# Moving the mixer's stages between the head slots of a fused attention, mixer and FFN kernel

## The chip, the cores and the metric

One core of one Trainium2 chip runs the whole program. The metric is the device time of one execution in microseconds; the profile gives the span from the program's first to its last instruction beside it. An execution is compared with another one of the same chip, and a time of several runs is their median.

## The reference, cut to what matters

2048 tokens of 576 features are normalized (xn) and go down two ways. Way A is attention of 32 heads over the last 512 keys of a cache, with an output projection. Way B is a mixer (layernorm, a product with w1, gelu, a shift of four column groups by one or two tokens, a product with w2, residual) and then an FFN of 4608 hidden features. The output is x + s · silu(B).

```
xn = _layernorm(x)
s  = attention(xn, k_cache, v_cache, wq, wo)          # 32 heads, 512 keys, softmax, then @ wo
h  = gelu(_layernorm(xn) @ w1)                        # mixer, first stage
hs = shift(h) @ w2                                    # mixer, last stage: groups shifted by 1, -1, 2, -2 tokens
x1 = xn + hs
h2 = gelu(_layernorm(x1) @ w3) @ w4                   # FFN
out = x + s * silu(x1 + h2)
```

## The kernel before, in words

The tokens are cut into four blocks of 512 (b = 0 to 3, NB = 4). The attention part runs through 128 slots, u = 32·b + head; the main loop from L742 on writes the order of TensorE, SyncE (SP) and GpSimd (POOL) out by hand (`manual_schedule` with these three engines). What VectorE (DVE) and ScalarE (ACT) do, and in which order, is set by the tile framework's planner, which also places instructions that stand outside of such a region into an engine's order where it finds them free to go; `high_priority` lifts some DVE and ACT work.

A slot u holds, in this order on TensorE: a score product `stage_s(u, 0)` (L459, 128x512), the query projection of the next head `stage_q(u+1)` (L439; in every fourth slot, `trip`, also four half products of `rest_q`, L425, and `stage_s(u, 1)` moves ahead of them), then what `fill[u]` holds, then three more rounds: `stage_s(u, i)`, half of `stage_v(u-1)` for i = 1 and 2 (eight products po of 129 columns, L476), and a third of the slot's list of extra matmuls, `pe_fill[u]`. At the slot's end `stage_t(u-1)` issues the DMA transpose of head u-1's output on SP (L489, o to oT). A slot with an empty `pe_fill` is called bare here.

Beside the heads a block needs these steps:

- `load_x` (POOL), `ln1_steps` (DVE, three steps a slot through `later`) and four DMA transposes `tr1` (SP, L392) that fill `xT_b[b % 2]`, which `stage_q` of the block's first head reads one slot ahead of the block.
- `ln2_steps` (DVE, writes `xnn_b`) and four DMA transposes `tr2` (SP, L392) that fill `xnnT`, the input of the mixer's first stage.
- `b1(b, c)`, c = 0 to 4: five matmuls each (L552, into ph), then a gelu of six DVE instructions with a tanh on ACT between them (L567 to L575). Chunk 4 also copies two border columns to and from the neighbouring block.
- `b2_shift` (DVE, L592), `b2(b, tt)`, tt = 0 to 3 (five matmuls each, L603, then a DVE add L614), and `b2_rem` (twenty matmuls of 64 columns, an add L628, and the store of the block's x1 to `x1_dram` on SP, L630).
- `wo_atoms(b)`: the block's output projection, five groups of matmuls over the 32 heads' oT (L500): four of 32 with 512 columns, one of 128 with 64 columns. Groups of blocks 0 to 2 lie in five slots of the next block, those of block 3 behind the last slot.
- `load_x1(0)`, `ln3_steps(0)` and `ln3_transpose(0)` (SP, L206): FFN's first layernorm, for block 0.

`x1_pool` has two buffers. They hold, one after another, key staging, x of blocks 2 and 3, the scaled attention output of blocks 0 to 2 on its way to `s_dram`, each block's x1 until its store, and the x1 that the FFN loads back (`load_x1`, L196). `xnn_b`, `xnnT`, `hs` and the gelu's three temporaries have one buffer each; `hb` has two, as have the banks `pq` that psq, ph and psx1r share.

The FFN (from L765 on) has TensorE, DVE and ACT ordered by hand. Its weight loads `load_w` (nine slabs of four DMAs on SP, L788 to L793) are tied behind the last head's transpose; `load_sx(0)` and `load_x1(1)` come after them in the program, and `ln3_work(1)`, the layernorm of FFN block 1, is handed out step by step to the DVE between the FFN's own steps (`pop`), from the first round on.

```
        with tc.issue_after(last_t[0].ins):
            for i in range(NSL):
                load_w(i)
...
        load_sx(0)
        load_x1(1)
        work = ln3_work(1)
```

Where the steps stood before, by slot (counted within 0 to 127; base = 32·b):

| step | block 0 | block 1 | block 2 | block 3 |
|---|---|---|---|---|
| ln2 from | 7 | 35 | 67 | 99 |
| tr2 | 28, 29, 30, 31 | 39, 39, 40, 40 | 71, 71, 72, 72 | 103, 103, 104, 104 |
| b1 chunks 0 to 4 | 33, 34, 36, 37, 38 | 42, 44, 45, 46, 48 | 74, 76, 77, 78, 80 | 106, 108, 109, 110, 112 |
| b2 tiles 0 to 3 | 50, 52, 53, 54 | 82, 84, 85, 86 | 114, 116, 117, 118 | 120, 121, 122, 124 |
| ln1 from (for that block) | before the loop | 19 | 55 | 87 |
| output projection | 34 to 38 | 65 to 69 | 97 to 101 | behind 127 |

ln3 of block 0 began in slot 121 and its transposes stood in slot 125.

Of the kernel before, what the change touches and what calls it, by code (L numbers as in the profile page):

```python
# [31 lines left out]
def kernel(  # L32
# [14 lines left out]
    nc = tc.nc  # L47
# [15 lines left out]
    NB = S // QB  # L63
# [140 lines left out]
    def ln3_transpose(b):  # L204
        for tt in range(TB):
            nc.sync.dma_start(out=xT_b[b % 2][:, :, tt * P:(tt + 1) * P], in_=xm_b[b % 2][:, tt, :], transpose=True)  # L206

    with ExitStack() as actx:
# [99 lines left out]
        def late(ap, fn):  # L308
            g = nc.gpsimd.tensor_copy(out=gate[:, :], in_=ap)
            with tc.issue_after(g.ins):  # L310
                fn()
# [272 lines left out]
        def b2_shift(b):  # L584
            with tc.high_priority(offset=HP):
                b2_shift_(b)
# [79 lines left out]
        def later(u, make, per):  # L666
            cell = []
            for i in range(2 * TB + 1):
                def step(i=i):
                    if not cell:  # L670
                        cell.append(make())
                    cell[0][i]()
                at(u + i // per, step)

        def trip(u):
            return Hq - 1 <= u < U - 1 and u % 4 == 3

        for b in range(NB):
            base = b * Hq
            if b > 0:  # L680
                for i, group in enumerate(wo_atoms(b - 1)):
                    pe(base + (2 if b == 1 else 1) + i, group)
            later(base + (7 if b == 0 else 3), lambda b=b: ln2_steps(b), 3)
            for tt in range(TB):
                at(base + (28 + tt if b == 0 else 7 + tt // 2), lambda b=b, tt=tt: tr2(b, tt))
            for c, u in enumerate((33, 34, 36, 37, 38) if b == 0 else (10, 12, 13, 14, 16)):
                pe(base + u, b1(b, c))
            for bb in ([b - 1] if b > 0 else []) + ([b] if b == NB - 1 else []):
                o2 = base + (24 if bb == b else 18)
                at(o2 - 1, lambda bb=bb: b2_shift(bb))  # L690
                tiles = [o2 + i for i in range(TB + 1) if not trip(o2 + i)][0:TB]
                for tt, u in enumerate(tiles):
                    pe(u, b2(bb, tt))
                pe(tiles[-1], b2_rem(bb))
            if b + 1 < NB:
                at(base + (14 if b == 0 else 4), lambda b=b: late(pT_t[b * Hq + (14 if b == 0 else 4)][0][0:1, 0:1],
                                                                 lambda: load_x(b + 1, nc.gpsimd)))
                u1 = base + (23 if b else 19)
                later(u1, lambda b=b: ln1_steps(b + 1), 3)
                for tt in range(TB):  # L700
                    at(u1 + (3 + tt // 2 if b else 5 + tt), lambda b=b, tt=tt: tr1(b + 1, tt))
# [17 lines left out]
        for b in range(NB):  # L719
            at((b + 1) * Hq + 1, lambda b=b: row_range(b))  # L720
        at(3 * Hq + 10, lambda: load_x1(0))
        later(3 * Hq + 25, lambda: ln3_steps(0), 3)
        at(3 * Hq + 29, lambda: ln3_transpose(0))
        at(U + 2, finish_flag)

        with tc.manual_schedule(engines={SP, POOL, PE}):
# [456 lines left out]
```

## Time and profile before

| | |
|---|---|
| median of 3 runs | 845.85 us (843.45, 845.85, 849.34) |
| the profiled execution's own time | 844.12 us |
| its span | 842.3 us |
| granted TensorE clock, mean | 0.999 |
| slots 0 to 127 | 11.4 to 517.7 us of the span |
| output projection of block 3 | 519.3 to 552.5 us |
| FFN | 552.5 us to the end |

In a line of the timeline stand the start in us, the time from the first start to the last end of the merged instructions, the engine, the line of the kernel, the operation, what it writes and reads, the count, and in brackets the idle time before it with what ended it. Consecutive instructions of one kind are one line. Matmuls overlap each other, so what one costs is read from one start to the next and not from its length. `SPq` and `POOLq` are issues of DMAs; the time of an issue is not that of its transfer. A line of windows gives the busy time of each engine in a stretch. DMA lines give the median time from issue to landing.

### The profile page before, as it was taken

Reading aid. Unit: us, or ns where it says so; the run is one execution under the profiler, and the core shown is the slowest. Engines: PE = TensorE matmul, PEld = TensorE weight load, DVE = VectorE, ACT = ScalarE, POOL = GpSimd, SP = SyncE. Lnnn points to the kernel's source line nnn. Section 1 sums busy time; section 2 is a strip of 40 time slices with the busy share of each in tenths; the row PEclk is TensorE's granted clock in tenths of the full one; section 3 lists DMA queues with packets and bytes.
Section 4 is the critical chain, followed back from the end, with each engine's and each line's share of the span. In section 5 each row is a group of like instructions: output and inputs, shape, how many; then the busy total and the mean of one; then the engine's idle time right before and its main releaser. Section 6 shows DMA issues by size and latency. Waiting matters only on the chain.

```text
span 842.3 us, 19541 instructions
## 1 busy us (share of the span) xinstructions
PE 827.3 (98%) x7971; PEld 476.4 (57%) x7971; DVE 474.0 (56%) x1430; ACT 451.3 (54%) x806; POOL 92.2 (11%) x157
## 2 busy tenths in 40 slices
PE   8999999999999999999999999999999999999997
PEld 5666654655664555565465555455555555555555
DVE  5878655568762458683448775034246636555333
ACT  6777753478793388794367865033233333334610
POOL 3242313001010110110011000000000000000000
PEclk9999999999999999999999999999999999999999
DMA  7997963263371183463065236993001321230101
GB/s 187 197 169 181 194 173 73 63 104 95 95 135 45 42 155 67 108 122 80 19 110 127 68 94 126 275 344 61 2 2 44 63 70 44 45 88 16 44 15 46
DMA packets 140752, 83.95 MB, mean 100 GB/s; under 512 B 107328, under 2 KB 133632, under 8 KB 140656
## 3 DMA queue, kind: packets, MB, share of 16 engines
q1 hardware_dynamic: 130048, 53.01, 30.7%
q0 software_dynamic: 9216, 28.15, 12.1%
q8 instruction: 64, 1.05, 0.6%
q10 hardware_dynamic: 1392, 1.48, 0.5%
q14 instruction: 32, 0.26, 0.1%
HBM read 49.17 MB, written 9.44 MB: 70 GB/s over the span
## 4 chain that ended last, share of the span: by engine, by line


## 5 line engine op out<-in xcount | busy, mean ns | idle before, releaser
L461 ACT ACTIVATE pT<-sc 128x512 bf16<-128x512 f32 x512 | 289.3, 597 | 127.3 <-PE sc L459 118.3
L459 PE MATMUL sc<-qT,kT 128*128 128x512 bf16 x512 | 178.5, 378 | 1.4 <-DVE qT L449 0.6
L476 PEld LDWEIGHTS <-pT 128*128 128x128 bf16 x2048 | 137.7, 98 | 55.3 <-issue 8.9
L476 PE MATMUL po<-v_sb,pT 128*128 128x129 bf16 x2048 | 162.0, 220 | 0.4 <-ACT pT L461 0.4
L439 PE MATMUL psq<-xT_b,wq_b 128*128 128x512 bf16 x544 | 138.3, 379 | 0.3 <-DVE xT_b L405 0.3
L834 PE MATMUL ph<-xT_b,w_s 64*128 64x512 bf16 x976 | 127.1, 376 | 0.0
L871 PE MATMUL pm<-w_s,h 64*128 64x512 bf16 x864 | 122.3, 377 | 0.0
L500 PE MATMUL pswo<-wo_sb,oT 128*128 128x512 bf16 x512 | 116.7, 379 | 1.6 <-DMA oT<-o 1.6
L481 DVE TENSOR_TENSOR o<-po,ri_b 128x256 bf16<-128x256 f32 x256 | 108.1, 422 | 6.6
L852 ACT ACTIVATE h<-ph 128x512 bf16<-128x512 f32 x67 | 39.4, 597 | 130.5 <-PE ph L834 130.5
L871 PEld LDWEIGHTS <-h 64*128 64x128 bf16 x1728 | 70.8, 94 | 55.5 <-issue 0.4
L500 PEld LDWEIGHTS <-oT 128*128 128x128 bf16 x1024 | 65.1, 98 | 58.0 <-DMA oT<-o 2.1
L871 PE MATMUL pr<-w_s,h 64*128 64x64 bf16 x864 | 90.2, 189 | 0.2 <-ACT h L852 0.2
L439 PEld LDWEIGHTS <-wq_b 128*128 128x128 bf16 x544 | 52.8, 97 | 64.0 <-issue 3.4
L834 PEld LDWEIGHTS <-w_s 64*128 64x128 bf16 x1152 | 57.1, 94 | 48.3 <-issue 0.2
L850 DVE COPY hx<-ph 128x512 f32<-128x512 f32 x55 | 38.0, 691 | 69.3 <-PE ph L834 69.3
L480 DVE RECIPROCAL ri_b<-po 128x2 f32<-128x2 f32 x256 | 42.7, 167 | 53.0 <-PE po L476 48.8
L449 DVE CAST qT<-psq 128x512 bf16<-128x512 f32 x56 | 38.6, 690 | 49.0 <-PE psq L425 29.4
L447 DVE TENSOR_TENSOR qT<-psq,rq 128x512 bf16<-128x512 f32 x48 | 33.2, 691 | 52.6 <-ACT pT L461 32.2
L459 PEld LDWEIGHTS <-kT 128*128 128x128 bf16 x512 | 47.3, 97 | 27.1 <-DVE qT L449 0.6
L264 POOL DMA_DIRECT2D wq_b<-in_A_wq_dram x30 | 23.3, 776 | 303.5 <-PE sc L459 275.0
L824 DVE TENSOR_SCALAR fence<-ph,ph 1x1 f32<-1x1 f32 x61 | 12.8, 209 | 49.7 <-PE ph L834 49.1
(146 smaller groups left out, 739.7 us busy)
## 6 DMA issues: line engine op xcount, KB each, us to landing
wq_b<-in_A_wq_dram POOLq DMA_DIRECT2D x30, 512.0 KB, 4.6
w_s<-in_B_w_dram SPq DMA_DIRECT2D x9, 576.0 KB, 7.1
wo_sb<-in_A_wo_dram POOLq DMA_DIRECT2D x8, 576.0 KB, 5.2
w_s<-in_B_w_dram SPq DMA_DIRECT2D x9, 512.0 KB, 7.2
x_dram<-x SPq DMA_DIRECT2D x4, 576.0 KB, 3.6
x<-x_dram SPq DMA_DIRECT2D x4, 576.0 KB, 4.8
s_b<-s_dram SPq DMA_DIRECT2D x4, 576.0 KB, 5.2
x_b<-in_A_x_dram SPq DMA_DIRECT2D x4, 576.0 KB, 6.1
```

The costliest lines, as they stand in the source:

```text
L439: nc.tensor.matmul(psq[:, :], lhsT=w[:, kc, hh * Dh:(hh + 1) * Dh], rhs=xT_b[qb % 2][:, kc, :], start=(kc == 0 and not (qb and hh == 1)), ...
L449: nc.vector.tensor_copy(out=qT[:, :], in_=psq[:, :])
L459: nc.tensor.matmul(sc[:, :], lhsT=kT[:, g, kc * P:(kc + 1) * P], rhs=qT_t[u][:, :], start=True, stop=True)
L461: nc.scalar.activation(out=pT[:, :], in_=sc[:, :], func=ACT.Exp, scale=SCALE)
L476: nc.tensor.matmul(po[:, j, :], lhsT=pTs[kc][:, tt * P:(tt + 1) * P], rhs=v_sb[:, g, kc, 0:Dh + 1], start=(kc == 0), stop=(kc == KCH - 1))
L480: nc.vector.reciprocal(out=ri, in_=po[:, :, Dh])
L481: nc.vector.tensor_tensor(out=o[:, t0:t0 + 2, :], in0=po[:, :, 0:Dh], in1=ri.unsqueeze(2).to_broadcast([P, 2, Dh]), op=ALU.mult)
L500: nc.tensor.matmul(ps, lhsT=oT_t[qb * Hq + h][:, tt, :], rhs=wo_sb[:, h, lo:hi], start=(h == 0), stop=(h == Hq - 1))
L834: nc.tensor.matmul(ps[i][:, :], lhsT=lhsT, rhs=xT[half, kc, :], start=first, stop=last, skip_group_check=True)
L850: nc.vector.tensor_copy(out=src[:, :], in_=ps[i][:, :])
L852: nc.scalar.activation(out=h3[:, :], in_=src[:, :], func=ACT.Gelu_apprx_tanh)
L871: nc.tensor.matmul(out, lhsT=h3_t[b, fc][half, tt * P:(tt + 1) * P], rhs=w4_s[fc // WS][half, fc % WS, lo:hi], start=key not in started, s ...
```

## The change

The arithmetic and all matmuls stay; only the slots change. `pe` gets three lists for the mixer's first stage and the output projection, so that a chunk can stand ahead of a projection group in its slot ("early") or behind it ("after"):

| step | block 0 | block 1 | block 2 | block 3 |
|---|---|---|---|---|
| ln2 from | 7 | 35 | 60 | 85 |
| tr2 | 27, 28, 29, 30 | 39, 39, 40, 40 | 63, 63, 64, 64 | 89, 89, 90, 90 |
| b1 chunks 0 to 4 | 34, 36, 36, 37, 37 | 44, 45, 46, 48, 49 | 65, 66, 66, 68, 68 | 97, 98, 98, 100, 100 |
| b2 tiles 0 to 3 | 52, 53, 54, 56 | 72, 73, 74, 76 | 104, 105, 106, 108 | 124, 125, 126, 127 |
| ln1 from (for that block) | before the loop | 19 | 56 | 80 |
| output projection | 34 to 38 | 65 to 69 | 97 to 101 | behind 127 |

tr1 of blocks 2 and 3 moves with ln1 (three and four slots behind its begin). In slot 27 the first tr2 now stands ahead of the last tr1 of block 1. ln3 of block 0 begins in slot 116 and its transposes stand in slot 120. The loads of x stay in slots 14, 36 and 68, `load_x1(0)` in slot 106.

```diff
+        ln2_at = (7, Hq + 3, 2 * Hq - 4, 2 * Hq + 21)
+        tr2_at = ((27, 28, 29, 30), (Hq + 7, Hq + 7, Hq + 8, Hq + 8),
+                  (2 * Hq - 1, 2 * Hq - 1, 2 * Hq, 2 * Hq), (2 * Hq + 25, 2 * Hq + 25, 2 * Hq + 26, 2 * Hq + 26))
+        b1_early = {Hq + 2: [(0, 0)], Hq + 4: [(0, 1)], Hq + 5: [(0, 3)]}
+        b1_after = {Hq + 4: [(0, 2)], Hq + 5: [(0, 4)]}
+        for b in range(2, NB):
+            base = b * Hq
+            b1_early.update({base + 2: [(b, 1)], base + 4: [(b, 3)]})
+            b1_after.update({base + 1: [(b, 0)], base + 2: [(b, 2)], base + 4: [(b, 4)]})
+        for c, u in enumerate((12, 13, 14, 16, 17)):
+            b1_after[Hq + u] = [(1, c)]
+        b2_at = ((Hq + 20, Hq + 21, Hq + 22, Hq + 24), (2 * Hq + 8, 2 * Hq + 9, 2 * Hq + 10, 2 * Hq + 12),
+                 (3 * Hq + 8, 3 * Hq + 9, 3 * Hq + 10, 3 * Hq + 12), (4 * Hq - 4, 4 * Hq - 3, 4 * Hq - 2, 4 * Hq - 1))
+        x_at = (14, Hq + 4, 2 * Hq + 4)
+        ln1_at = (19, Hq + 24, 2 * Hq + 16)
...
+        for u, chunks in b1_early.items():
+            for b, c in chunks:
+                pe(u, b1(b, c))
+        for b in range(1, NB):
+            for i, group in enumerate(wo_atoms(b - 1)):
+                pe(b * Hq + (2 if b == 1 else 1) + i, group)
+        for u, chunks in b1_after.items():
+            for b, c in chunks:
+                pe(u, b1(b, c))
...
-        later(3 * Hq + 25, lambda: ln3_steps(0), 3)
-        at(3 * Hq + 29, lambda: ln3_transpose(0))
+        later(3 * Hq + 20, lambda: ln3_steps(0), 3)
+        at(3 * Hq + 24, lambda: ln3_transpose(0))
```

The loop over the blocks below it keeps its calls of `later`, `at` and `pe` and takes their slots from these tables.

More of the change, by code (lines that the diff above doesn't have):

```diff
@@ L676, in trip @@
             return Hq - 1 <= u < U - 1 and u % 4 == 3
-        for b in range(NB):
[L679 to L683, printed above, removed]
-            for tt in range(TB):
[L685 to L694, printed above, removed]
+        ln2_at = (7, Hq + 3, 2 * Hq - 4, 2 * Hq + 21)
@@ new lines @@
+        for b in range(1, NB):
[4 more added lines that the diff above has]
+                pe(u, b1(b, c))
+        for b in range(NB):
+            later(ln2_at[b], lambda b=b: ln2_steps(b), 3)
+            for tt in range(TB):
+                at(tr2_at[b][tt], lambda b=b, tt=tt: tr2(b, tt))
+            at(b2_at[b][0] - 1, lambda b=b: b2_shift(b))
+            for tt in range(TB):
+                pe(b2_at[b][tt], b2(b, tt))
+            pe(b2_at[b][TB - 1], b2_rem(b))
@@ L695 @@
             if b + 1 < NB:
-                at(base + (14 if b == 0 else 4), lambda b=b: late(pT_t[b * Hq + (14 if b == 0 else 4)][0][0:1, 0:1],
-                                                                 lambda: load_x(b + 1, nc.gpsimd)))
-                u1 = base + (23 if b else 19)
+                at(x_at[b], lambda b=b: late(pT_t[x_at[b]][0][0:1, 0:1], lambda: load_x(b + 1, nc.gpsimd)))
+                u1 = ln1_at[b]
                 later(u1, lambda b=b: ln1_steps(b + 1), 3)
```

## The prediction, made before the change was run

> **What bounds the kernel now.** I read the page's first part, then the timeline of TensorE (PE) for its idle places, then SP's queue and the DVE around each of them.
>
> ```profile
> span 842.3 us, 19541 instructions
> PE 827.3 (98%) x7971; PEld 476.4 (57%) x7971; DVE 474.0 (56%) x1430; ACT 451.3 (54%) x806; POOL 92.2 (11%) x157
> ```
>
> TensorE is busy for 98% of the span, and the change keeps every matmul. So it can only win the time in which PE waits, and it can lose wherever it makes PE wait anew. The 98% alone wouldn't prove that, since matmuls overlap; the starts do. In the timeline of PE, below, one line with eight po products is followed 0.47 us later (516.97 to 517.44) by a score product, and that one 0.21 us later by the next. These are the undisturbed steps against which I read the waits.
>
> [...]
>
> ```profile
> 110.50 0.63 PE L476 MATMUL po<-v_sb,pT 128*128 128x129 bf16 x8
> 112.70 0.38 PE L552 MATMUL ph<-xnnT,w_sb 128*128 128x512 bf16 x1 [1.57 <-DMA xnnT<-xnn_b]
> ...
> 174.23 0.63 PE L476 MATMUL po<-v_sb,pT 128*128 128x129 bf16 x8
> 175.96 0.39 PE L552 MATMUL ph<-xnnT,w_sb 128*128 128x512 bf16 x1 [1.10 <-DMA xnnT<-xnn_b]
> ...
> 180.57 0.63 PE L476 MATMUL po<-v_sb,pT 128*128 128x129 bf16 x8
> 181.29 0.86 PE L459 MATMUL sc<-qT,kT 128*128 128x512 bf16 x2
> ...
> 314.48 0.86 PE L459 MATMUL sc<-qT,kT 128*128 128x512 bf16 x2
> ...
> 447.48 0.86 PE L459 MATMUL sc<-qT,kT 128*128 128x512 bf16 x2
> ...
> 516.04 0.88 PE L476 MATMUL po<-v_sb,pT 128*128 128x129 bf16 x8
> ...
> 516.97 0.63 PE L476 MATMUL po<-v_sb,pT 128*128 128x129 bf16 x8
> 517.44 0.38 PE L459 MATMUL sc<-qT,kT 128*128 128x512 bf16 x1
> 517.65 0.49 PE L476 MATMUL po<-v_sb,pT 128*128 128x129 bf16 x3
> 518.50 0.94 PE L476 MATMUL po<-v_sb,pT 128*128 128x129 bf16 x13 [0.36 <-ACT pT L461]
> 519.28 1.02 PE L500 MATMUL pswo<-wo_sb,oT 128*128 128x512 bf16 x4
> ...
> 524.67 1.03 PE L500 MATMUL pswo<-wo_sb,oT 128*128 128x512 bf16 x4
> 527.33 1.04 PE L500 MATMUL pswo<-wo_sb,oT 128*128 128x512 bf16 x4 [1.63 <-DMA oT<-o]
> ```
>
> From these starts: chunk (0,0) in slot 33 waits 1.73 us (112.70 less 110.97) for the transposes of xnnT; chunk (1,0) in slot 42 waits 1.26; slot 43 loses 0.25 before its third score product and 0.28 before its fourth, and slots 75 and 107 show the same long pair of score products (0.86 where an undisturbed pair takes 0.59), 0.53 each time; the last slot loses 0.25 and 0.67, together 0.92, to ACT's exps; and the last projection waits 1.80 (527.33 less 525.53) for the last head's oT. Together 7.3 us are there to be won.
>
> **The change part by part.**
>
> Block 0's first stage. tr2 goes one slot earlier, chunk (0,0) one slot later (34), so PE comes for xnnT about 2.7 us later, a bare slot (four of them, one longer, take the 11.31 us of the window below), and would come 0.9 us after the data even if the transposes landed no sooner. The 1.73 us go. The price is on SP: in slot 27 the first tr2 passes ahead of the last tr1, which `stage_q(32)` needs in slot 31. One issue is 1.3 us (2.52 for two, below). I take 0, as that transpose is issued four slots ahead; bounds 0 and 1.3.
>
> Block 1. Chunk (1,0) goes from slot 42 to 44 behind the same transposes, so PE comes over 5 us later than before: the 1.26 us go. Slot 43's 0.53 goes as well: there the tanh of a chunk that ended slot 42 sat in ACT's order ahead of two copies that free score banks. Now the chunk in slot 44 has no `trip` slot behind it. Chunk (1,2) in 46 has one (47), as chunk (1,3) had before; I take 0.1 for it, bounds 0 and 0.53.
>
> Blocks 2 and 3. The first stage goes into projection slots of about 10 us, where PE has 32 long matmuls beside it: a late tanh no longer meets a short slot. The 0.53 us of slots 75 and 107 go. Eleven gelu chains of DVE and ACT move from bare to long slots and cost nothing there: 32 projection matmuls, 6.9 us, cover each. POOL issues the same loads in the same slots as before.
>
> The price of that is in front of slot 65, where ln1(2), tr1(2), ln2(2) and tr2(2) now follow each other between slots 56 and 64. Two lines of windows (the third engine is the DVE), then of the timeline of SP and PE, and the landing times of xnnT's transposes:
>
> ```profile
> 225.23:250.50 25.27, 25.27 (x226) 15.54 (x225) 19.54 (x75) 23.20 (x44) 4.00 (x6) 1.00 0.67 127
> 239.19:250.50 11.31, 11.31 (x102) 6.83 (x101) 6.69 (x20) 10.27 (x20) 1.98 (x3) 1.00 0.78 134
> ```
>
> ```profile
> 233.71 2.52 SPq L392 DMA_TRANSPOSE xT_b<-xn_b  x2
> ...
> 237.63 3.58 SPq L392 DMA_TRANSPOSE xT_b<-xn_b  x2
> ```
>
> ```profile
> 244.96 0.59 PE L439 MATMUL psq<-xT_b,wq_b 128*128 128x512 bf16 x2
> ```
>
> ```profile
> DMA to landing us min/median/max: 2.6/3.6/8.7
> ```
>
> Bare slots alone keep the DVE busy 6.69 of 11.31 us, so nine of them leave about 10 us (25.27 x 0.41). The whole stretch with most of ln1(2) took 19.54, that is 4.6 more, and ln2 is about as long. Both fit, just; each ends late, and SP, which takes its queue in order, holds the heads' transposes behind tr1 and tr2 meanwhile. Before, the last tr1(2) was issued at 238.9 and, at 3.6 us, landed 2.4 us ahead of the 244.96 of `stage_q(64)`. One slot later that margin is gone, save for some 1.5 us that ln1's start gains since slot 56 has no qT cast on the DVE. I take 0.2 us of waiting there and 0.1 for oT(63), which now queues behind tr2(2) but is needed only at the end of slot 65; bounds 0 and 1.5 together.
>
> Last stages. b2 tiles move between bare slots for nothing. In slot 127 the tile and the 20 small products give PE 1.65 us of other work while ACT catches up. The last exp can't end before some 1.06 us after its score product starts (517.44 to 518.50), and PE has 0.65 us to fill it: 0.4 us stay of 0.92, so 0.5 is won.
>
> The end, on SP. Before, ln3's four transposes and a 576 KB load stood in front of the last heads' transposes:
>
> ```profile
> 511.48 0.36 SPq L630 DMA_DIRECT2D x_dram<-x  x1
> ...
> 514.21 5.23 SPq L206 DMA_TRANSPOSE xT_b<-xnn_b  x4
> ...
> 520.85 0.53 SPq L196 DMA_DIRECT2D x<-x_dram  x1
> 521.50 4.12 SPq L489 DMA_TRANSPOSE oT<-o  x3
> 525.71 0.53 SPq L788 DMA_DIRECT2D w_s<-in_B_w_dram  x1
> ...
> 559.68 0.37 SPq L793 DMA_DIRECT2D w_s<-in_B_w_dram  x1
> ...
> 560.93 0.37 SPq L803 DMA_DIRECT2D s_b<-s_dram  x1
> ```
>
> ```profile
> x_dram<-x SPq DMA_DIRECT2D x4, 576.0 KB, 3.6
> ```
>
> ```profile
> s_b<-s_dram SPq DMA_DIRECT2D x2, 576.0 KB, 7.1
> ```
>
> With ln3's transposes five slots earlier SP has no backlog, and the last oT goes out about 2 us after the projection's start, W (519.28 before). It is needed 6.7 us after W (31 x 0.216), so the 1.80 us go, even beside the x1 store that now lies just ahead.
>
> But that store is block 3's x1, now at the end of slot 127 instead of 124, and `load_x1(1)` needs its buffer: of the two, one holds block 0's x1 until the FFN is done with it. Before, the load found its place at 520.85, after the store had landed and before the weights were released. Now the store, issued about at W, lands at W + 3.6, and the weights are released by the last transpose at about W + 2.8. They stand ahead of the load in the program, and the trace shows all 36 of them unbroken (525.71 to 559.68) with s_b behind them. So I expect the load behind the weights. s_b was issued 35.2 us after the first weight and took 7.1: that gives a landing at W + 45.1. Without the load in front of the weights they run up to 1.9 us earlier (576 of 1152 KB in a slab's 3.8 us), so W + 43.2 to 45.1; I take W + 44.0. Who waits:
>
> ```profile
> 552.53 1.04 PE L834 MATMUL ph<-xT_b,w_s 64*128 64x512 bf16 x8
> ...
> 557.94 0.44 DVE L151 BATCH_NORM_STATS2 ln_st<-x 128x6 f32<-128x288 bf16 x1
> 560.02 0.69 DVE L850 COPY hx<-ph 128x512 f32<-128x512 f32 x1 [1.65 <-PE ph L834]
> ...
> 560.77 1.04 PE L834 MATMUL ph<-xT_b,w_s 64*128 64x512 bf16 x8
> ```
>
> The FFN's DVE order is by hand: the first statistics of ln3(1) stand at 557.94, and hx behind them, which frees the bank that PE fills from 560.77. The FFN starts at W + 31.4 (33.25 less 1.80). So the DVE stops at W + 36.9, PE at W + 39.7, and PE goes on 1.1 us (0.44 and 0.69) after the landing: a hold of 44.0 + 1.1 - 39.7 = 5.4 us. Bounds: 0, if the load goes ahead of the weights, and 6.5.
>
> [...] All waits above are under 2 us and the clock stayed at full speed through them. [...]
>
> Sum: won 1.73 + 1.26 + 3 x 0.53 + 0.5 + 1.80 = 6.9; lost 0.1 + 0.3 + 5.4 = 5.8. The profiled execution took 844.1 us, so 843.0. The median shown is 1.7 above that execution; I put the forecast midway, 0.9 up: 843.9 us.
>
> **The rivals.**
>
> The load isn't held: the planner gets it in among the first weights, because it tracks another buffer or a sooner landing. For it speaks that before it stood ahead of them; against it the unbroken 36. Then 844.1 - 6.9 + 0.4 = 837.6, and 838.5 on the scale above.
>
> Slower: the load comes behind s_b and x_b too. s_b waits for the last store of the projection:
>
> ```profile
> s_dram<-hb ACTq DMA_DIRECT2D x1, 576.0 KB, 7.8
> ```
>
> That store goes out half a us after the projection's end, so s_b at W + 31.4 + 0.5 + 7.8 = W + 39.7, the load some 0.9 later, and it lands 7.1 after that at W + 47.7: a hold of 9.1, so 846.7, and 847.6. The point from which the change loses is a landing after W + 45.1, where the hold eats the whole 6.5. For it speaks that s_b stands first in the program; against it that s_b's data come only at the projection's end, when the load has long been free.
>
> The hold cools the clock:
>
> ```profile
> 1.58 4.02 PE L732 MATMUL warm<-ident 128*128 128x128 bf16 x36 [1.58 <-POOL ident masks.py:199]
> ```
>
> At the start a 128-column product takes 107 ns ((4.02 - 0.29)/35) and a 129-column po later 59. A cold stretch of 4 to 5 us after the hold would cost about 2.4: 845.4, and 846.3. [...]
>
> The load goes ahead of the last transpose and makes it wait for the store: the load would go out at about W + 3.8 and oT land 6.5 later, as before (520.85 to 527.33), at W + 10.3; PE waits 3.6 there instead of 1.8, but the FFN has its x1 in time: 844.1 - 6.9 + 3.6 + 0.4 = 841.2, and 842.1. Against it: the last transpose needs nothing of the store and is ready first.
>
> The change doesn't do what it says: tr2 of a block still lands late, since the DVE or SP is late by as much as the slots gained. For it speaks the full DVE in slots 56 to 64. It would leave 1.5 to 3 us of the waits: about 845.5.
>
> **How the numbers follow.** Forecast 0.50; load not held 0.20; load behind s_b 0.08; cooled clock 0.08; load ahead of the last transpose 0.07; waits not gone 0.07. The range takes the unheld load at its low end (838.5, less 1.5 for two medians' scatter) and the slower ones at the high end (847.6 and 0.8 us): 837.0 to 848.4; the forecast's own is 842 to 846. 1%, about what a measurement of this kernel can tell from no change, is 8.5 us: 837.4 and 854.3. All cases lie within; only the unheld load comes near, so faster 0.09, same 0.85, slower 0.06 for a wait that I don't see.
>
> **What would show it.** PE without idle time before L552 in slots 34 and 44 and before L459 in 75 and 107; none at L500 half-way through the first projection group; L196 behind the last L793 on SP; a DVE wait at L151 and a PE gap of about 5 us some 8 us into the FFN. Wrong would be: L196 ahead of L788; a gap at L439 in slot 63 over 1.5 us; PEclk under 9 in the FFN.

## The result, and the profile after the change

| | before | after |
|---|---|---|
| median of 16 executions each | 846.35 us (843.45 to 852.74) | 838.19 us (837.10 to 843.39) |
| ratio after to before | | 0.9898, 95% interval 0.9877 to 0.9918 |
| the profiled execution's own time | 844.12 us | 837.62 us |
| its span | 842.3 us | 835.8 us |
| start of block 3's projection, W | 519.28 | 514.02 (see below) |
| start of the FFN | 552.53 | 545.77 |

The kernel became 1.0% faster (0.8 to 1.2%), just at the bound of 1% beyond which the prediction gave "faster" a chance of 0.09. The time lies within its range of 837.0 to 848.4, but its likeliest case, 843.9 with an own range of 842 to 846, did not come; what came is its rival "the load isn't held" (838.5, a chance of 0.20). Its own first sign of being wrong, L196 ahead of L788, came too (L788 is L803 in the changed kernel).

First the two windows behind the last slot, of the kernel before and of the changed one (start and end, length, busy time of PE, PEld, DVE, ACT and POOL, granted clock, DMA share, GB/s):

```profile
519.30:552.50 33.20, 31.57 (x259) 16.18 (x256) 2.09 (x11) 2.39 (x4) 1.69 (x2) 1.00 0.99 264
552.50:842.30 289.80, 283.36 (x3355) 157.89 (x3351) 136.13 (x367) 100.54 (x170) 0.00 (x0) 1.00 0.21 58
```

```profile
514.00:545.80 31.80, 31.52 (x259) 16.29 (x261) 2.13 (x11) 2.39 (x4) 1.69 (x2) 1.00 1.01 260
545.80:836.00 290.20, 283.20 (x3348) 157.98 (x3351) 136.03 (x367) 100.51 (x170) 0.00 (x0) 0.99 0.22 61
```

The trace of the changed kernel lacks 86 of the 7971 matmul records; a missing 512-column product shows as one extra step of 0.216 us. The projection's first product is one of them: the first one recorded starts at 514.24, so W is put one step earlier.

The FFN takes about as long as before (290.0 us against 289.8 from its start to the span's end), the projection 1.5 us less (31.75 against 33.25), and 5.3 us come from the slots. So next to nothing was given back in the FFN. The order on SP and the DVE's first statistic of ln3(1) in the FFN, both of the changed kernel, say why:

```profile
513.31 0.36 SPq L630 DMA_DIRECT2D x_dram<-x  x1
513.79 2.99 SPq L489 DMA_TRANSPOSE oT<-o  x2
517.46 0.38 SPq L196 DMA_DIRECT2D x<-x_dram  x1
517.93 0.73 SPq L803 DMA_DIRECT2D w_s<-in_B_w_dram  x1
```

```profile
551.18 0.44 DVE L151 BATCH_NORM_STATS2 ln_st<-x 128x6 f32<-128x288 bf16 x1
```

`load_x1(1)` (L196) stands ahead of the first weight and not behind the 36th. It took 8.2 us and landed at 525.7, so the first statistic at 551.18 finds its data 25 us old, and no brackets with a wait stand behind it.

Now the waits of TensorE, each as the time between two starts less the undisturbed step and less the step of a missing record, in both profiled executions:

| place | before | after |
|---|---|---|
| first chunk of blocks 0, 1, 2, 3, for xnnT (slots 33, 42, 74, 106 before) | 1.74, 1.27, 0.30, 0.11 | 0, 0, 0, 0 |
| slots 43, 75, 107, score banks behind a tanh | 0.52, 0.52, 0.52 | 0, 0, 0 |
| slots 47, 79, 111, the same | 0.36, 0.36, 0.36 | 0.45, 0, 0 |
| slot 51, the same | 0 | 0.53 |
| a bare slot at 359.6 | 0 | 0.08 |
| slot 127, ACT's exps | 0.92 | 0.42 |
| block 3's projection, oT | 1.80 | 0.29 |
| sum | 8.78 | 1.77 |

The difference, 7.0, fits what the starts show: the FFN starts 6.76 us earlier though the first score product starts 0.12 us later (11.54 against 11.42), which makes 6.9. Rows of TensorE's timeline after the change: chunk (0,0) at 113.76 and chunk (1,0) at 179.08 follow eight po products after the undisturbed 0.47 us; slot 51 shows a new wait (203.83 to 204.90, where slot 55 takes 0.53 from 218.89 to 219.42); the last rows are slot 127's wait and the FFN's first product.

```profile
113.29 0.63 PE L476 MATMUL po<-v_sb,pT 128*128 128x129 bf16 x8
113.76 1.02 PE L552 MATMUL ph<-xnnT,w_sb 128*128 128x512 bf16 x3
...
178.61 0.63 PE L476 MATMUL po<-v_sb,pT 128*128 128x129 bf16 x8
179.08 0.38 PE L552 MATMUL ph<-xnnT,w_sb 128*128 128x512 bf16 x1
...
203.83 0.39 PE L425 MATMUL psq<-xT_b,wq_b 64*128 64x512 bf16 x2
204.10 0.86 PE L425 MATMUL sc<-xT_b,wq_b 64*128 64x512 bf16 x2
204.90 0.64 PE L476 MATMUL po<-v_sb,pT 128*128 128x129 bf16 x8
...
218.89 0.39 PE L425 MATMUL psq<-xT_b,wq_b 64*128 64x512 bf16 x2
...
219.42 0.64 PE L476 MATMUL po<-v_sb,pT 128*128 128x129 bf16 x8
...
513.25 0.94 PE L476 MATMUL po<-v_sb,pT 128*128 128x129 bf16 x13 [0.25 <-ACT pT L461]
...
545.77 1.04 PE L849 MATMUL ph<-xT_b,w_s 64*128 64x512 bf16 x8
```

ACT in slot 51 of the changed kernel shows what the new wait ended with: a tanh first, then three exps, and only then the two copies (rq). The second of these exps ends at 204.54, and TensorE's last half product, which needs a score bank, starts at 204.59. So here the tanh delays the exps that free the banks; in slot 43 before, it delayed the copies.

```profile
202.94 0.63 ACT L573 ACTIVATE g_th<-g_u 128x512 bf16<-128x512 bf16 x1 [0.33 <-DVE g_u L571]
203.48 1.55 ACT L461 ACTIVATE pT<-sc 128x512 bf16<-128x512 f32 x3
204.91 1.09 ACT L430 ACTIVATE rq<-sc 128x512 f32<-128x512 f32 x2
```

Two things stay to be explained: whether the hold of 5.4 us was wrong as a mechanism or only did not arise, and why the medians differ by 8.2 us when the two profiles differ by 6.5.

### The profile page after: what moved, and what is told of

Read it like the earlier page. It is cut to its first block, busy times and chain, and to the rows that moved or that the text cites. A ratio compares the mean times of both kernels' runs of the same rounds, so it can differ in the third digit from the quotient of the medians.

```text
span 835.8 us, 19469 instructions
## 1 busy us (share of the span) xinstructions
PE 820.3 (98%) x7885; PEld 475.9 (57%) x7971; DVE 473.8 (57%) x1430; ACT 452.9 (54%) x806; POOL 91.8 (11%) x157
## 4 chain that ended last, share of the span: by engine, by line
## 5 line engine op out<-in xcount | busy, mean ns | idle before, releaser
L459 PE MATMUL sc<-qT,kT 128*128 128x512 bf16 x493 | 169.0, 378 | 0.9 <-DVE qT L449 0.6
L439 PE MATMUL psq<-xT_b,wq_b 128*128 128x512 bf16 x509 | 134.3, 379 | 2.1 <-DVE xT_b L405 0.3
```

Source lines behind the costliest of these rows:

```text
L439: nc.tensor.matmul(psq[:, :], lhsT=w[:, kc, hh * Dh:(hh + 1) * Dh], rhs=xT_b[qb % 2][:, kc, :], start=(kc == 0 and not (qb and hh == 1)), ...
L459: nc.tensor.matmul(sc[:, :], lhsT=kT[:, g, kc * P:(kc + 1) * P], rhs=qT_t[u][:, :], start=True, stop=True)
```

## The experiments

Every ratio is to the kernel before on the same chip.

### The front alone, and the tail alone

e1_front is the changed kernel with the tail as before:

```diff
-(4 * Hq - 4, 4 * Hq - 3, 4 * Hq - 2, 4 * Hq - 1))
+(3 * Hq + 24, 3 * Hq + 25, 3 * Hq + 26, 3 * Hq + 28))
-        later(3 * Hq + 20, lambda: ln3_steps(0), 3)
-        at(3 * Hq + 24, lambda: ln3_transpose(0))
+        later(3 * Hq + 25, lambda: ln3_steps(0), 3)
+        at(3 * Hq + 29, lambda: ln3_transpose(0))
```

> The tail is as before: block 3's last stage in slots 120, 121, 122 and 124, the FFN's first layernorm in slots 121 and 125. Only the stages between the slots 27 and 108 stand as in the changed kernel. Theory: the waits inside the slots are independent of those of the tail. The starts of TensorE show 6.1 us of them before in slots 33 to 111 and 1.3 us after, so this kernel is 4.8 us shorter than the kernel before (ratio 0.994); the last slot's 0.92 us and the projection's wait for oT of 1.80 us stay. Rival: the tail's transposes are paced by something that doesn't move with the heads, so that the wait in the projection grows by what was won (ratio 0.998 or above).

Measured: median 842.07 us, ratio 0.9949 (0.9915 to 0.9982); the profiled execution took 844.20 (span 842.4). The median is what the theory expected, the profile is its rival (a span as long as before). TensorE's timeline in block 3's projection, two windows there, and SP's DMAs (KB, us to landing) of e1_front:

```profile
514.54 6.21 PE L500 MATMUL pswo<-wo_sb,oT 128*128 128x512 bf16 x28
523.72 1.11 PE L500 MATMUL pswo<-wo_sb,oT 128*128 128x512 bf16 x2 [2.97 <-DMA oT<-o]
525.13 5.10 PE L500 MATMUL pswo<-wo_sb,oT 128*128 128x512 bf16 x12 [0.29 <-DMA oT<-o]
```

```profile
520.00:524.00 4.00, 1.03 (x5) 0.24 (x3) 0.00 (x0) 0.00 (x0) 1.10 (x1) 0.88 1.13 127
524.00:528.00 4.00, 3.71 (x9) 1.14 (x9) 0.02 (x1) 0.60 (x1) 0.00 (x0) 0.50 1.12 226
```

```profile
x<-x_dram SPq DMA_DIRECT2D x1, 576.0 KB, 6.2
oT<-o SPq DMA_TRANSPOSE x3, 5.8
```

The heads' data are 5 us earlier, but the last oT only 3.6 (the first of the three lands at 523.67, before it was 527.28): the wait grew from 1.80 to 3.1 us, and the granted clock is 0.50 from 523.1 to 529.9. Twelve products stand in 5.10 us, about 0.43 each instead of 0.216. Most of the front's gain was spent here. It isn't in every execution: six of the twelve took 838.8 to 840.2 us at a mean clock of 0.997 to 0.999, the other six 843.9 to 850.3 at 0.994 to 0.997. None lies near the median, so that it agrees with the theory is luck.

e2_tail is the kernel before with the tail alone moved:

```diff
-                o2 = base + (24 if bb == b else 18)
+                o2 = base + (28 if bb == b else 18)
```

and ln3's two lines as in the change.

> The kernel before, with only the tail changed: block 3's last stage in slots 124 to 127, the FFN's first layernorm in slots 116 and 120. Theory: the projection's wait for oT goes from 1.80 us to about 0.3, and the last slot's from 0.92 to 0.4: 2.0 us shorter (ratio 0.9976), and load_x1(1) stands ahead of the weights on SP, as in the changed kernel. Rival: the tail only wins beside an early first stage, since SP's queue is late from the slots before; then the wait for oT stays over 1 us and the ratio over 0.999. A second rival, that the tail is worth more than its waits (the time between the medians is 8.2 us, the spans differ by 6.5): ratio under 0.996.

Measured: 843.06 us, ratio 0.9960 (0.9937 to 0.9983). TensorE's timeline in slots 33 and 42 and in the projection:

```profile
113.16 0.38 PE L552 MATMUL ph<-xnnT,w_sb 128*128 128x512 bf16 x1 [2.11 <-DMA xnnT<-xnn_b]
...
176.96 0.39 PE L552 MATMUL ph<-xnnT,w_sb 128*128 128x512 bf16 x1 [1.64 <-DMA xnnT<-xnn_b]
...
520.24 12.03 PE L500 MATMUL pswo<-wo_sb,oT 128*128 128x512 bf16 x54
```

The projection runs without a gap and the last slot keeps 0.42, as expected. The ratio stands at the bound of the second rival (under 0.996), with an interval that holds the theory's 0.9976 too, so the two are not told apart. The span, 841.7, is above the expected 840.3 since the two waits for xnnT, untouched here, are 0.5 us longer each in this execution than in the first profile of the kernel before (brackets 2.11 and 1.64 against 1.57 and 1.10). In these profiles the waits that end with a DMA's landing differ from one execution to the next; those on ACT are the same to 0.01 us (the last slot's bracket is 0.25 here and in the changed kernel, and 0.36 or 0.35 in the two profiles of the kernel before, in e1, e7, e9 and e10).

### What made the last oT late

The prediction put the wait of 1.80 us down to ln3's transposes and the 576 KB load together. Three kernels take them apart. e7_front_load_behind_oT is e1_front with one line more:

```diff
-        load_x1(1)
+        with tc.issue_after(last_t[0].ins):
+            load_x1(1)
```

> e1_front with one thing changed: load_x1(1) goes out behind the last head's transpose on SP and not ahead of the last three. ln3's four transposes stay in slot 125 and block 3's last stage in 120 to 124. In e1_front the last three oT were issued at 516.79, 518.42 and 519.72 and landed at 523.67, 524.18 and 525.08, right behind the load's 522.57, and PE waited 3.1 us and then ran at half its steps for 6 us. Theory B (the load in front): the three go out 0.5 us earlier and land 2.5 us behind their issue as the ones before them did, at about 518.8, 520.1 and 521.4, PE comes for them at 520.6, 520.8 and 521.0, so the wait is 0.4 us and no step doubles: some 5.5 us less than e1_front's profile (842.4), 837. Theory A (SP's backlog of ln3's transposes): the wait stays over 2 us and the time within 2 us of e1_front's.

Measured: 837.89 us, ratio 0.9904 (0.9870 to 0.9939), span 835.5: theory B. The DMA line of the three last transposes and the projection in its timeline:

```profile
oT<-o SPq DMA_TRANSPOSE x3, 3.0
```

```profile
514.37 8.82 PE L500 MATMUL pswo<-wo_sb,oT 128*128 128x512 bf16 x40
```

5.8 us to landing became 3.0, the wait is gone, and so is the half clock. SP's backlog of ln3's transposes is still there (5.24 us of issues from 509.07 on) and costs nothing.

e9_ln3_early_only is the changed kernel with block 3's last stage back in slots 120 to 124, e4_ln3_late the changed kernel with ln3 back in slots 121 and 125 (each undoes one line of the tail).

> The changed kernel with block 3's last stage back in slots 120, 121, 122 and 124; ln3 stays in slots 116 and 120. load_x1(1) then stands ahead of the last three transposes of heads again, as before the change, but nothing else delays SP there, so it goes out when the store of block 3's x1 has landed, several us ahead of them. Theory A (backlog): the wait for oT is gone (under 0.5 us), the last slot's 0.92 us is back: 0.5 us slower than the changed kernel's 835.8, span 836.3. Theory B (a load in front of the last transposes): it has 4 us more of lead than in e1_front, so part of the delay stays, a wait of 0.5 to 2 us: 837 to 838.

> The changed kernel, but the FFN's first layernorm of block 0 back in slots 121 and 125; block 3's last stage stays in slots 124 to 127, load_x1(1) stays behind the last head's transpose on SP. Theory A (SP's backlog makes the last oT late): ln3's four transposes take SP 5.2 us in the last slots, the last two transposes of heads go out 3 us or more after those of the changed kernel (513.79 and 515.59), and PE waits 2 to 4 us half-way into the first projection group; above about 3 us the steps behind it are doubled for some us as in e1_front (3.35 us of gap, then 0.43 us a step). Time 839 to 843. Theory B (the 576 KB load in front of the last transposes makes them land late): the load is behind them here, so the wait stays near the changed kernel's 0.3 and the time at 838.

Measured: e9 838.02 us, ratio 0.9903 (0.9877 to 0.9929), span 835.9, no wait for oT; the load is ahead of the last three transposes, but out at 510.97, and has landed at 515.4, five us before TensorE comes for them. e4: 838.44 us, ratio 0.9906 (0.9879 to 0.9933), span 837.3, a wait of 0.24; ln3's four transposes are late and the load is behind (theory B again; of the 1.5 us above the changed kernel's span, 0.3 are a later first product, 0.5 a wait for xnnT in slot 34 of this execution and 0.5 lie in the FFN). So the wait needs both things before the change: the backlog pushes the load to a place just in front of the last transposes, and there the load delays their landing. Either half of the tail's move takes it away.

The 0.29 us that stay in the changed kernel have another ground, which is open. Its last oT is issued at 515.59, 1.9 us ahead of the load, and yet lands only at 520.95, 5.4 us later. The store of block 3's x1 goes out 2.3 us ahead of it and lands 4.3 us before it. The last two oT have a median of 4.6 us there, and of 4.1 in e2 and 4.5 in e4, where that store stands in the same slot; in e7 and e9, where it goes out at 506.36 and 506.07, 9 us and more ahead of the last oT, the last three have 3.0 and 2.9.

e10_before_load_behind_oT asks the kernel before, with the same line as in e7 and nothing else:

> The kernel before with one thing changed: load_x1(1) goes out behind the last head's transpose on SP and not ahead of the last three. All slots are as before. Theory (the load in front of the last transposes makes both the wait of 1.80 us in the projection and, in executions in which that wait passes about 3 us, the half-speed steps behind it): the wait is under 0.3 us in the profile, the span 1.6 us below 842.3, 840.7, and the runs scatter less: none of them over 845, a clock of 0.997 or more in each, so that the median falls by more than the 1.6 us, some 3 us (ratio 0.996). Rival (the scatter comes from the waits for xnnT in slots 33 and 42, or from elsewhere): the runs still reach 848 and more at a clock of 0.996 or less, and the median falls by 1.6 us at the most (ratio 0.998).

Measured: 843.52 us, ratio 0.9974 (0.9955 to 0.9994), span 841.2. In the timeline half of the wait stays (0.94 us where the theory had under 0.3), since the backlog's last transpose is issued at 523.87 and lands 2.8 us later:

```profile
519.07 6.85 PE L500 MATMUL pswo<-wo_sb,oT 128*128 128x512 bf16 x31
526.69 2.55 PE L500 MATMUL pswo<-wo_sb,oT 128*128 128x512 bf16 x11 [0.77 <-DMA oT<-o]
```

The ratio, 0.9974, lies nearer to the rival's 0.998 than to the theory's 0.996, which the quotient of the two medians gives (843.52 and 846.82). The theory's claim on the scatter was too strong: four of twelve executions are still over 845 (up to 849.77, at a clock of 0.994), so a part of the scatter comes from elsewhere, as the rival had it.

e12_before_again is the kernel before, profiled once more.

> The kernel before once more, for a second profile of it on another chip. Theory: where its time lies above the first profile's 844.1 us, the surplus is in the waits that end with a DMA's landing (1.74 us in slot 33, 1.27 in slot 42, 0.30 in 74, 0.11 in 106 and 1.80 in block 3's projection in the first profile), and in doubled steps of TensorE behind one of them that passes 3 us; the waits on ACT (0.25 to 0.53 us each) are the same to 0.01 us. Rival: the surplus is spread over all steps, or lies in the FFN.

Measured: 847.99 us, span 846.2. Its projection, the window behind the wait, and the DMA lines of the load and the three transposes behind it:

```profile
519.56 6.42 PE L500 MATMUL pswo<-wo_sb,oT 128*128 128x512 bf16 x29
528.92 16.39 PE L500 MATMUL pswo<-wo_sb,oT 128*128 128x512 bf16 x67 [2.94 <-DMA oT<-o]
```

```profile
529.00:533.00 4.00, 4.00 (x11) 1.41 (x12) 0.00 (x0) 0.60 (x1) 0.94 (x1) 0.57 0.87 247
```

```profile
x<-x_dram SPq DMA_DIRECT2D x1, 576.0 KB, 7.5
oT<-o SPq DMA_TRANSPOSE x3, 6.0
```

The load took 7.5 us here and 6.1 in the first profile; the wait is 3.1 us instead of 1.80, and the clock is halved for 3.4 us, from 0.5 us after the wait's end on. The wait's 1.3 us more and the cold steps' 1.7 make 3.0 of the 3.9 us between the two spans; 0.5 lie ahead of the first score product and 0.6 in the FFN, and the waits for xnnT are 0.2 shorter together. The waits on ACT are equal. That is likely where much of the 1.7 us between the two differences lies: the profile that the prediction was made from was one of the kernel's better executions (844.12, the median is 846.35), and the change took away a wait that is longer in others. e10 points the same way, since it lowers the median by 3.3 us and the span by 1.1; one profile of a slow execution doesn't show it for the rest. Not all of it: three of the changed kernel's 16 executions also have a mean clock of 0.997 or less (838.24, 839.85 and 843.39 us), and which wait of theirs does it isn't known.

### The hold that didn't come

e3_load_behind_weights makes the order that the prediction expected, with the load behind the 36th weight and ahead of s_b:

```diff
-        load_sx(0)
-        load_x1(1)
+        with tc.issue_after(last_w[0].ins):
+            load_x1(1)
+        with tc.issue_after(last_x[0].ins):
+            load_sx(0)
```

(`last_w` and `last_x` hold the last weight's DMA and the load's.) e5_load_behind_s_x is the same without the last two lines, `load_sx(0)` staying first.

> The changed kernel with load_x1(1) put behind all 36 weight loads on SP, ahead of s_b and x_b: the order that the prediction took for the likeliest. Theory (the hold): TensorE stops at about W + 40.0 (W is the start of block 3's projection; in the changed kernel hx ends at 553.95 and the product behind it starts at 554.00, W is 514.0) and goes on 1.1 us after the load's landing. By the prediction's own landing, W + 44.0, that is 5.4 us more than the changed kernel; by the changed kernel's weights (37.1 us from the first to the last issue, beginning some 1.8 us earlier without the load's wait for the store, and 7 to 8 us for a 576 KB load) the landing is nearer to W + 47 and the hold 8 us. Rival 1: other work covers it, 0 to 1 us. Rival 2: the idle time also cools the clock, then TensorE's products behind the gap start at steps of about 0.4 us instead of 0.2 for a few us, and the time is 2.4 us above what the gap itself gives.

> The changed kernel with load_x1(1) behind the weights and behind s_b and x_b too: the order of the prediction's slower rival, there at a landing of W + 47.7 and a hold of 9.1 us. Theory (the hold): s_b leaves after its data have landed (the store landed at 555.04, W + 41.0, in the changed kernel), the load some 0.9 us later and beside two other loads, with a landing about W + 50 to 51 and a hold of 11 to 12 us, some 3 us more than with the load ahead of s_b; PE's gap is as long as the lateness of the landing, one for one. Then this kernel is slower than the kernel before (ratio 1.005). Rival 1: covered, 0 to 1 us. Rival 2: the longer gap cools the clock: 2.4 us more than the gap itself, with TensorE's steps doubled behind it.

Measured: e3 847.63 us, ratio 1.0017 (0.9989 to 1.0045), span 847.0; e5 850.73 us, ratio 1.0046 (1.0016 to 1.0077), span 848.5. The DVE's and TensorE's timelines of e3, then two windows of it:

```profile
560.94 0.46 DVE L151 BATCH_NORM_STATS2 ln_st<-x 128x6 f32<-128x288 bf16 x1 [9.46 <-DMA x<-x_dram]
```

```profile
554.18 0.20 PE L889 MATMUL pr<-w_s,h 64*128 64x64 bf16 x2
562.04 1.89 PE L852 MATMUL ph<-xT_b,w_s 64*128 64x512 bf16 x8 [7.67 <-DVE hx L868]
```

```profile
557.00:562.00 5.00, 0.00 (x0) 0.00 (x0) 1.06 (x3) 0.00 (x0) 0.00 (x0) 0.53 1.03 347
562.00:567.00 5.00, 4.96 (x32) 2.18 (x33) 1.79 (x7) 0.63 (x1) 0.00 (x0) 0.50 0.89 293
```

The mechanism is as the prediction had it: the load landed at 560.92, TensorE went on 1.1 us later (562.04). The gap is 7.8 us, and from there to the end the kernel takes 3.2 us more than the changed kernel from the same product (847.0 - 562.04 against 835.8 - 554.00). The half clock over 5.5 us made 2.7 of them: ACT's 20th gelu of the FFN behind that product comes 42.3 us after it, and 39.6 in the changed kernel. In e5 the landing is 3.2 us later, the gap 11.6 us, and the cold part costs only 1.1 (40.7), since the clock comes back 2.6 us after the products do. So both the theory and rival 2 hold, rival 2 with a size that differs from its 2.4.

d1_rem_behind_last_slot lets the planner choose, with the last products of block 3's last stage, and so the store of its x1, later:

```diff
-            pe(b2_at[b][TB - 1], b2_rem(b))
+            if b < NB - 1:
+                pe(b2_at[b][TB - 1], b2_rem(b))
...
         for i, group in enumerate(wo_atoms(NB - 1)):
             pe(U + 1 + i, group)
+        pe(U + 1, b2_rem(NB - 1))
```

> The changed kernel with one step later by one place: the twenty small products of block 3's last stage, the add and the store of its x1 stand at the head of block 3's output projection and not at the end of slot 127, so the store goes out about 2 us later. Nothing is tied by hand; in this program the planner puts the store behind the first weight load and load_x1(1) behind all 36 weights, s_b and x_b on SP. Theory (the hold of the prediction, and of e5_load_behind_s_x, 848.5 us of span with a landing at W + 50.1): the same landing, the DVE stops at its first statistic of ln3(1), PE waits about 11 us and runs at half its steps for 2.5 to 6 us behind that: 848 to 851. Rival (the hold in e5 came from the forced order's other effects, as on the s_b and x_b of the first FFN block): under 842.

The expectation is wrong on what this does: `pe(U + 1, ...)` puts the products behind the first group of the projection, not ahead of it. They run at 520.19, some 8 us later than in the changed kernel. The planner put the add (L628) behind steps of the DVE that wait for another small DMA until 524.16, so the store goes out at 525.23, 12 us later and not 2.

Measured: 854.93 us, ratio 1.0096 (1.0066 to 1.0127), span 854.2. SP, the DVE and TensorE of it:

```profile
515.57 0.52 SPq L805 DMA_DIRECT2D w_s<-in_B_w_dram  x1
525.23 0.37 SPq L630 DMA_DIRECT2D x_dram<-x  x1
```

```profile
524.80 0.41 DVE L628 TENSOR_TENSOR x<-psx1r,xn_b 128x256 bf16<-128x256 f32 x1
...
567.78 0.46 DVE L151 BATCH_NORM_STATS2 ln_st<-x 128x6 f32<-128x288 bf16 x1 [16.71 <-DMA x<-x_dram]
```

```profile
520.19 0.28 PE L603 MATMUL psx1r<-w_sb,hb 128*128 128x64 bf16 x4
...
568.88 1.86 PE L851 MATMUL ph<-xT_b,w_s 64*128 64x512 bf16 x7 [14.71 <-DVE hx L867]
```

Without any tie the load went behind the weights and the first s_b and x_b (558.89), and the hold came, 15 us of it: SP stood in front of the store for 9 us (516.09 to 525.23), which made the weights late as well, more than the theory had. So the danger that the prediction saw is real. In the changed kernel the twenty products stand at slot 127's end, one projection group ahead of the place where it comes.

### Block 1's first stage

e8_b1_spaced moves block 1's chunks away from the slots ahead of 47 and 51, and with them block 0's last stage:

```diff
-        for c, u in enumerate((12, 13, 14, 16, 17)):
+        for c, u in enumerate((11, 12, 15, 16, 19)):
-        b2_at = ((Hq + 20, Hq + 21, Hq + 22, Hq + 24),
+        b2_at = ((Hq + 21, Hq + 22, Hq + 24, Hq + 25),
```

> The changed kernel with block 1's first stage in slots 43, 44, 47, 48 and 51 (it was 44, 45, 46, 48, 49) and block 0's last stage in 53, 54, 56 and 57. Theory: what the changed kernel still loses in slots 47 (0.45 us) and 51 (0.53 us) is ACT's order: a gelu's tanh that comes about 3 us behind its chunk stands ahead of the two copies that free banks in every fourth slot (43, 47, 51). A chunk in such a slot or in the one behind it has its tanh in the next two, so both waits go: 1.0 us off the span (834.8). Rival: the waits are the DVE's lateness and follow the chunks to other slots, or the first chunk in slot 43 comes for its input before it has landed (as slot 42 did before, 1.27 us): no gain or up to 1 us lost.

Measured: 845.49 us, ratio 1.0001 (0.9986 to 1.0016), span 843.0: 7.2 us lost. The waits of slots 47 and 51 went as expected, one of 0.38 came in slot 59, and in slot 63 TensorE waited for the last two transposes of xT (TensorE, SP and POOL of e8, then SP and POOL of the changed kernel):

```profile
247.28 1.87 PE L439 MATMUL psq<-xT_b,wq_b 128*128 128x512 bf16 x4 [5.13 <-DMA xT_b<-xn_b]
```

```profile
231.54 0.37 SPq L630 DMA_DIRECT2D x_dram<-x  x1
...
240.37 2.60 SPq L392 DMA_TRANSPOSE xT_b<-xn_b  x2
```

```profile
240.43 0.79 POOL L264 DMA_DIRECT2D wq_b<-in_A_wq_dram  x1 [9.71 <-PE sc L459]
```

```profile
225.88 0.37 SPq L630 DMA_DIRECT2D x_dram<-x  x1
...
236.50 3.48 SPq L392 DMA_TRANSPOSE xT_b<-xn_b  x2
```

```profile
240.63 0.78 POOL L264 DMA_DIRECT2D wq_b<-in_A_wq_dram  x1 [9.34 <-PE sc L459]
```

In the changed kernel the last two transposes of xT went out at 236.50 and 238.75, ahead of a 512 KB weight load, and the later one landed at 241.43, 0.8 us before `stage_q(64)` comes. In e8 they went out beside that load and landed at 246.1 and 247.0, and the clock was halved from 245.3 to 252.1.

What made them late is the store of block 0's x1 (L630). The planner put its last add (L628) behind a row of ln1(2) on the DVE, to 231.10, four us after the products it adds; SP waited 7.2 us for it (from 224.30 on), and from the store at 231.54 on it issued one DMA behind the other until it came to the two at 240.37 and 241.69. In the changed kernel that add stands at 225.43 and the store at 225.88. The rows of ln1(2) weren't late: the last one ends at 234.42 in e8 and at 235.62 in the changed kernel.

e11_b1_spaced_b2_kept keeps block 0's last stage in its slots and takes (11, 12, 15, 16, 17) for the chunks. Its expectation still puts the lateness down to ln1(2).

> The changed kernel with block 1's first stage in slots 43, 44, 47, 48 and 49 and block 0's last stage where the change put it (52, 53, 54, 56). In e8_b1_spaced the chunks' spacing took the waits of slots 47 and 51 away, but the last stage one slot later made ln1(2) late, whose rows overwrite what block 0's last add reads; the last two transposes of xT came behind a weight load and PE waited 5.1 us for them in slot 63. Theory: with the last stage kept, xT lands 0.8 us ahead of PE again, as in the changed kernel (241.43 against 242.19); the wait of slot 47 (0.45 us) goes, that of slot 51 (0.53) stays for the chunk in slot 49: span 0.4 us below 835.8. Rival: the DVE's work of block 1 itself (a chunk later on average by half a slot) is what made ln1(2) late; then PE waits in slot 63 again, 3 us or more, and its steps double: 840 or more.

Measured: 838.38 us, ratio 0.9901 (0.9875 to 0.9927), span 836.4. No wait in slot 63, 0.16 in 47, 0.53 in 51, about as the theory had it, and the store of block 0's x1 is back at 225.87; the sum of such small waits can't be told from the changed kernel by the time. No version here beats the changed kernel by more than the scatter.

## Why the prediction was right or wrong, point by point

- **The waits for xnnT** (1.73 and 1.26): right, both gone in the profile (in e4's execution 0.5 us of one is there, in slot 34). The prediction missed two more of the same kind, 0.30 in slot 74 and 0.11 in slot 106, which went too.
- **ACT's order**, 3 x 0.53 won and 0.1 lost: the three went. Missed were 3 x 0.36 in slots 47, 79 and 111, of which two went. Lost were 0.09 more in slot 47, as much as was taken for it, and 0.53 in slot 51, a slot that the prediction didn't name. What was left out on the two sides partly cancels, by luck: 6.5 without the hold was forecast, 6.9 from the first score product to the FFN measured.
- **tr2 ahead of the last tr1, and the full DVE ahead of slot 65**, 0 and 0.3: 0 measured. As a price of lateness there the bound of 1.5 us was far too small, though: e8 shows 5.3 us of wait and the halved clock for transposes that are 3 to 4 us later. The bound counted the DVE's lateness, and neither a store in front of the transposes on SP nor the next load beside them.
- **The last slot**, 0.5 won: 0.50 measured.
- **The oT wait**, 1.80 won: 1.51 measured. The ground given, SP's backlog, was half of it (e7, e9, e10).
- **The hold**, 5.4: this step failed, and with it the likeliest time. "So I expect the load behind the weights" compared W + 3.6 for the store's landing with W + 2.8 for the last transpose. The store went out at 513.31, W - 0.7, and landed 3.4 us later at W + 2.7; the last transpose's issue took from W + 1.6 to W + 2.8; the load was put between it and the weights and issued at W + 3.4. So the two instants lie 0.1 us apart, and the other way round. An order that the planner makes can't be read off two estimated instants 0.8 us apart. What it compares isn't in a trace; seen is that it put the load ahead of the weights in all kernels of this study that left it the choice with the store in its place, and behind them in d1, where the store's products stand a projection group later. Why it changes there is open.
- **The size of the hold**, had it come: 10.5 us in e3's profile (7.8 of gap and 2.7 of cold steps; 9.4 by the medians of e3 and the changed kernel) and not 5.4. The stop (W + 39.7) and the 1.1 us behind the landing were right (554.2 is W + 39.7 in e3, 562.04 is 1.1 behind 560.92); the landing was W + 46.4 and not W + 44.0, and the cooled clock, a rival with 2.4 us, took 2.7. The two belong together: none of the three holds in these runs (7.8 us in e3, 11.6 in e5, 15 in d1) came without the half clock. That a hold cools the clock was the author's guess, and the 2.4 an estimate from the products at the kernel's start (107 ns against 59): the longest waits of the profile before, 1.63 us for oT and 1.57 for xnnT, kept the granted clock at 1.00. What the runs show is a clock of 0.50 for 10.2 us with e3's gap of 7.8 us, and for 3.4 and 6.8 us with idle times of no more than 2.9 and 3.0 us (e12, e1).
- **Between profile and median**, 0.9 us: the sum for the unheld load was 837.6 on the profile's scale, and the profiled execution took 837.62. That they agree so closely is luck, as terms of 0.1 to 0.7 us that the sum lacked or had too high stand on both sides. On the medians the change wins 1.7 us more, likely since the kernel before loses more in the projection in other executions than in the one that was profiled (e12 is one).

## What to carry to other kernels

Where an order is left to a planner, put the two orders side by side as cases of their own with near-equal chances, or tie the order by hand; here twenty small products, and with them one store, a projection group later turn 1.0% faster into 1.0% slower. A wait for a small transfer is priced by what may stand in front of it on its queue, a bulk load or a store whose data come late, and not by its own lateness: here 3.1 us with the load in front (e1_front) and 5.3 with the late store (e8). A wait of TensorE that can come near 3 us is priced with the half clock beside it: in these profiles idle times up to 2.11 us (e2) kept the granted clock at 1.00, and with those of 2.94 (e12) and 2.97 us (e1) and the longer ones (e3, e5, e8, d1) it was 0.50 for 3.4 us and more. A profile is one execution: waits that end with a landing are the ones to allow a spread for (that for oT was 1.80 us in one execution of the kernel before and 3.1 in another).

## What the runs showed of the hardware

**The transposes beside bulk loads.** In the profiles before and after the change a quarter of the 128 oT transposes land within 2.43 us of their issue, and the soonest after 2.40. In e1_front the three issued from 516.79 to 519.72 landed from 523.67 to 525.08, behind the load's 522.57 that was issued 0.5 us ahead of the first of them; in e8 two landed 5.4 to 5.7 us after their issue beside a load of 512 KB that POOL had issued and that took 5.5 us. A load in front isn't the only thing that makes one late: the changed kernel's last oT took 5.4 us without one, for an open reason.

**The clock's stretches.** The granted clock was 0.50 for 3.4 us in e12, 6.8 in e1 and e8, 10.2 in e3 and e5 and 17.0 in d1; within 0.1 us the longer ones are two, three and five times the shortest. In these six runs it fell 2.3 (e1) to 3.6 us (e5) after TensorE's last product had ended (in e12 after 3.5 us, when the next ones already ran) and came back 2.6 (e5) to 6.2 us (e1) after the products went on; so a gap of 11.6 us (e5) cost less in cold steps, 1.1 us, than one of 3.1 us (e1_front), some 2.3.
